# Fills ahead of the loads, 80-row loads, and batch 1's P v as 128-column matmuls, in a sparse attention with an ELU network behind it

## The chip, the cores and the metric

The kernel runs on one core of a Trainium2 chip. The metric is the time of one execution in microseconds (us) on the device, the median of the runs shown; less is better. The engines of the core are called PE (matmul; PEld is its weight load), DVE (elementwise), ACT (activation functions), POOL and SP; the last two issue most DMAs here.

## What is computed

Inputs are q, k and v, each (8, 8, 576, 64) in float32 (batch, head, position, channel), and two weight matrices of 512 x 2048 and 2048 x 512. The output is (4608, 512) in float32.

```python
stride = 32
scores = scale * np.matmul(q, k.transpose(0, 1, 3, 2))
mask_local   = (rel >= 0) & (rel < stride)                    # heads 0..3
mask_strided = (rel >= 0) & (pos[None] % stride == pos[:, None] % stride)   # heads 4..7
attn = softmax(np.where(masks, scores, -1e9))
x = np.matmul(attn, v).transpose(0, 2, 1, 3).reshape(4608, 512)
h = x @ w_in
g = np.where(h > 0, h, np.exp(np.minimum(h, 0)) - 1)          # ELU
out = g @ w_out
```

## The kernel before

Everything stays in SBUF as bf16. Attention is worked batch by batch (0 to 7). The four local heads are called `l`, the four strided ones `s`; a key such as `1s0` means batch 1, strided, pair 0, and each pair has two halves `u`. Positions are taken in eight residues s of 72 places p each (position 8p + s), so a load of one head brings 72 rows of 8 x 64 numbers. Strided scores are then 72 x 72 blocks, local ones 128 x 96 blocks (32 earlier keys and 96 own).

The network works on chunks of 512 tokens, of which there are nine. L1 gives for each of 16 blocks m four matmuls into one bank of PSUM (128 x 512), then ACT takes exp (`h`), DVE or ACT clamps it (`i`, `j`), and DVE takes the larger of that and h (`g`). L2 gives for each of four blocks of 128 tokens 16 matmuls in four parts (`Z`), then a copy out of PSUM (`o` on ACT, `q` on DVE) and the store (`t`).

The order of all work is a string of tokens, ORDER, written out by hand or by a planner; each token calls one function, and every engine takes its instructions in that order. Tokens that matter here:

- `F` fills (masks, zero pads, ones), `K` casts of the first two strided heads of batch 0 from a float32 stage, `T` transposes on PE for batches 0 to 2 (NPE = 3) with copies `c` (DVE) or `C` (ACT);
- `S` scores, `e` exp, `m` mask, `O` P v, `n` log of the row sums, `r` their reciprocal by exp, `x` the product into xT;
- `a`, `b` the two halves of an L1 block in chunk 0, `L` a whole one;
- `D` loads on POOL's queue, which also cast float32 to bf16; `V` copies the last 32 rows of each block of v for the local heads, `W` copies v for the strided heads into `vsp`;
- `X` DMA transposes and `P` pad copies into `kp` on SP's queue, from batch 3 on.

P v has two forms, chosen by OLDPV. The old one (batches 0 and 1) works with 64-column weights: for each half two matmuls with a block of ones for the row sums, and eight or six with v, the two heads of a pair in the two halves of the array; sums and products stand in two banks, 128 x 288 each. The new one (batches 2 to 7) works with 128-column weights in which 64 columns of v stand beside 64 columns of ones, so that one matmul gives products and sums together: 64 x 576 each. Its weights are `vsp` (strided) and `vl` (local, two buffers in turn); their ones are written once by the fills `F.vs`, `F.v0`, `F.v1`. They come as tokens at the head of ORDER, after the loads of batch 0 have been issued in the program's text; the fill of `vl0` therefore comes after the load into `vl0`.

Batch 1's raw rows are loaded into regions that are not in use yet, the tail of xT and part of g[1] (`raw1`). Batches from 3 on are transposed by DMA over 80 rows (RP), so rows 72 to 79 of the raw buffers must hold something finite; before, three small loads (`D.fqs`, `D.fks`, `D.fql`) put it there.

Of the kernel before, what the change touches and what calls it, by code (L numbers as in the profile page):

```python
# [8 lines left out]
F32 = mybir.dt.float32  # L9
BF16 = mybir.dt.bfloat16  # L10
# [5 lines left out]
S = 576  # L16
# [15 lines left out]
OLDPV = (0, 1)  # L32
# [3 lines left out]
w.7.42 F.ks0 F.ks1 F.kl0 F.v1 F.vs F.v0 F.kl1 F.ms K.q.1 F.ml D.wi0.0 K.q.0 K.k.0 D.wi1.0 T.0s0.q.0  # L36
K.k.1 c.0s0.q T.0s0.k.7 D.wi2.0 T.0s1.q.6 c.0s0.k c.0s1.q D.wi3.0 S.0s0.1.01 S.0s0.0.23 e.0s0.1
T.0s1.k.7 e.0s0.0 m.0s0.1 c.0s1.k m.0s0.0 S.0s1.1.67 S.0s1.0.01 D.qs.1 e.0s1.1 O.0s0.1.23 e.0s1.0
D.ks.1 m.0s1.1 O.0s0.0.67 n.0s0.1 m.0s1.0 T.0l0.q.0 r.0s0.1 n.0s0.0 x.0s0.1 O.0s1.1.45 r.0s0.0
c.0l0.q D.vs.1 T.0l0.k.3 x.0s0.0 n.0s1.1 r.0s1.1 T.0l1.q.6 c.0l0.k T.0l1.k.7 x.0s1.1 C.0l1.q D.ql.1  # L40
V.0 S.0l0.1.01 S.0l0.0.56 c.0l1.k e.0l0.1 O.0s1.0.34 e.0l0.0 m.0l0.1 S.0l1.0.01 n.0s1.0 m.0l0.0
O.0l0.1.56 e.0l1.0 D.kl.1 r.0s1.0 m.0l1.0 S.0l1.1.01 n.0l0.1 x.0s1.0 e.0l1.1 O.0l0.0.34 r.0l0.1
m.0l1.1 O.0l1.0.01 x.0l0.1 n.0l0.0 O.0l1.1.56 r.0l0.0 D.vl.1 n.0l1.0 x.0l0.0 a.0.1.7 r.0l1.0 n.0l1.1
x.0l1.0 a.0.0.4 r.0l1.1 a.0.3.0 x.0l1.1 b.0.1 D.wo0.0 b.0.0 h.0.1 b.0.3 h.0.0 i.0.1 a.0.7.5 h.0.3
g.0.1 a.0.4.6 j.0.0 b.0.4 i.0.3 a.0.8.7 g.0.3 D.wo1.0 h.0.4 a.0.12.3 i.0.4 b.0.12 g.0.0 a.0.13.0
h.0.12 b.0.13 D.wo2.0 g.0.4 a.0.14.4 h.0.13 i.0.12 b.0.14 g.0.12 j.0.13 T.1s1.q.6 a.0.6.1 D.wo3.0
c.1s1.q h.0.14 b.0.8 g.0.13 a.0.9.6 h.0.8 i.0.14 b.0.7 D.fqs.0 g.0.14 j.0.8 a.0.2.0 b.0.9 h.0.7
g.0.8 a.0.5.4 h.0.9 i.0.7 a.0.10.3 D.fks.0 i.0.9 b.0.6 g.0.7 a.0.15.7 h.0.6 b.0.2 g.0.9 D.fql.0
b.0.15 h.0.2 i.0.6 b.0.10 g.0.6 h.0.15 b.0.5 h.0.10 i.0.2 T.1s0.k.6 T.1s0.q.5 i.0.15 D.qs.2 h.0.5
T.1l0.q.1 i.0.10 C.1s0.q a.0.11.2 g.0.15 b.0.11 C.1l0.q g.0.2 T.1s1.k.7 h.0.11 T.1l0.k.5 g.0.10  # L50
T.1l1.k.0 C.1s0.k i.0.5 T.1l1.q.1 D.ks.2 C.1l0.k i.0.11 Z.0.1.0.3 c.1l1.k C.1l1.q C.1s1.k g.0.11
S.1l1.1.56 S.1s0.0.01 e.1l1.1 g.0.5 Z.0.3.0.7 e.1s0.0 m.1l1.1 V.1 D.ql.2 S.1s1.0.45 S.1s1.1.01
e.1s1.0 Z.0.1.1.3 m.1s0.0 e.1s1.1 m.1s1.0 O.1l1.1.45 m.1s1.1 O.1s1.0.01 n.1l1.1 Z.0.3.1.7 r.1l1.1
n.1s1.0 D.kl.2 x.1l1.1 Z.0.1.2.3 r.1s1.0 x.1s1.0 O.1s1.1.45 Z.0.3.2.7 n.1s1.1 r.1s1.1 O.1s0.0.01
x.1s1.1 D.vs.2 Z.0.1.3.3 n.1s0.0 r.1s0.0 D.vl.2 S.1l0.1.45 o.0.1 x.1s0.0 Z.0.3.3.7 e.1l0.1 t.0.1
S.1l1.0.01 m.1l0.1 o.0.3 S.1s0.1.23 S.1l0.0.45 Z.0.0.0.6 e.1l1.0 t.0.3 e.1l0.0 m.1l1.0 O.1l0.1.01
Z.0.0.1.6 e.1s0.1 m.1l0.0 n.1l0.1 m.1s0.1 O.1l0.0.23 r.1l0.1 O.1s0.1.45 x.1l0.1 n.1l0.0 Z.0.0.2.6
n.1s0.1 r.1l0.0 r.1s0.1 Z.0.0.3.6 x.1l0.0 x.1s0.1 O.1l1.0.01 o.0.0 T.2s1.k.2 W.2 Z.0.2.0.3 n.1l1.0
t.0.0 r.1l1.0 c.2s1.k Z.0.2.1.3 x.1l1.0 V.2 L.1.2.0 L.1.1.1 h.1.2 i.1.2 L.1.0.2 h.1.1 g.1.2 L.1.8.4
i.1.1 h.1.0 g.1.1 j.1.0 L.1.5.0 h.1.8 g.1.0 L.1.4.1 h.1.5 i.1.8 i.1.5 L.1.6.2 h.1.4 g.1.8 Z.0.2.2.3  # L60
i.1.4 h.1.6 g.1.5 j.1.6 Z.0.2.3.3 g.1.4 g.1.6 T.2s1.q.0 o.0.2 L.1.7.1 c.2s1.q t.0.2 S.2s1.0.23 h.1.7
T.2s0.k.0 T.2s0.q.4 e.2s1.0 i.1.7 T.2l1.q.5 D.qs.3 c.2s0.q C.2s0.k L.1.3.6 g.1.7 C.2l1.q D.ks.3
m.2s1.0 S.2s0.0.34 h.1.3 T.2l1.k.5 D.vs.3 e.2s0.0 O.2s1.0.01 i.1.3 L.1.9.7 c.2l1.k n.2s1.0 m.2s0.0
L.1.11.2 r.2s1.0 g.1.3 h.1.9 O.2s0.0.34 x.2s1.0 h.1.11 T.2l0.q.6 T.2l0.k.5 n.2s0.0 i.1.9 D.ql.3
c.2l0.q L.1.15.0 r.2s0.0 g.1.9 L.1.10.1 i.1.11 h.1.15 x.2s0.0 C.2l0.k S.2s0.1.67 g.1.11 S.2s1.1.34
h.1.10 L.1.14.5 X.ks.3 i.1.15 e.2s0.1 i.1.10 D.kl.3 e.2s1.1 L.1.13.2 g.1.15 h.1.14 g.1.10 S.2l1.1.34
h.1.13 L.1.12.0 i.1.14 X.qs.3 m.2s0.1 j.1.13 g.1.14 O.2s0.1.67 e.2l1.1 Z.1.0.0.1 g.1.13 n.2s0.1
D.vl.3 m.2l1.1 P.s.3 h.1.12 S.2l0.0.23 S.2l1.0.45 m.2s1.1 Z.1.0.1.1 r.2s0.1 i.1.12 e.2l1.0 g.1.12
Z.1.0.2.1 e.2l0.0 x.2s0.1 O.2s1.1.45 m.2l0.0 O.2l1.1.23 n.2s1.1 S.2l0.1.67 W.3 Z.1.0.3.1 n.2l1.1
X.kl.3 m.2l1.0 r.2s1.1 Z.1.1.0.0 o.1.0 x.2s1.1 Z.1.1.1.0 r.2l1.1 D.qs.4 X.ql.3 e.2l0.1 x.2l1.1  # L70
O.2l0.0.45 D.ks.4 Z.1.1.2.0 n.2l0.0 m.2l0.1 D.vs.4 O.2l0.1.67 r.2l0.0 S.3s1.0.23 t.1.0 Z.1.2.0.1
n.2l0.1 x.2l0.0 e.3s1.0 Z.1.1.3.0 r.2l0.1 m.3s1.0 O.3s1.0.23 x.2l0.1 o.1.1 S.3s1.1.45 Z.1.2.1.1
n.3s1.0 t.1.1 e.3s1.1 O.2l1.0.67 Z.1.3.0.0 r.3s1.0 m.3s1.1 P.l.3 n.2l1.0 x.3s1.0 O.3s1.1.45
Z.1.3.1.0 X.ks.4 r.2l1.0 n.3s1.1 S.3s0.0.23 x.2l1.0 Z.1.3.2.0 e.3s0.0 r.3s1.1 L.2.8.6 m.3s0.0
x.3s1.1 L.2.4.7 h.2.8 D.ql.4 i.2.8 O.3s0.0.45 h.2.4 L.2.10.2 g.2.8 n.3s0.0 i.2.4 L.2.2.3 h.2.10
g.2.4 r.3s0.0 L.2.9.6 i.2.10 h.2.2 g.2.10 L.2.5.7 D.kl.4 h.2.9 i.2.2 x.3s0.0 j.2.9 L.2.1.2 g.2.2
h.2.5 S.3l1.0.45 g.2.9 h.2.1 L.2.11.3 e.3l1.0 i.2.5 i.2.1 L.2.6.6 h.2.11 D.vl.4 g.2.5 X.kl.4
S.3l0.1.45 g.2.1 h.2.6 L.2.7.7 i.2.11 e.3l0.1 i.2.6 L.2.14.2 m.3l1.0 h.2.7 m.3l0.1 O.3l1.0.45 g.2.6
h.2.14 Z.1.3.3.0 g.2.11 n.3l1.0 L.2.15.6 i.2.7 r.3l1.0 i.2.14 g.2.7 o.1.3 L.2.0.3 h.2.15 x.3l1.0
t.1.3 L.2.3.7 h.2.0 i.2.15 g.2.14 O.3l0.1.45 h.2.3 L.2.13.0 g.2.15 n.3l0.1 i.2.3 L.2.12.2 i.2.0  # L80
r.3l0.1 g.2.3 h.2.13 Z.1.2.2.1 x.3l0.1 h.2.12 S.3l1.1.67 i.2.13 S.3l0.0.45 e.3l1.1 g.2.0 Z.1.2.3.1
X.ql.4 e.3l0.0 g.2.13 S.3s0.1.67 o.1.2 Z.2.1.0.3 m.3l1.1 m.3l0.0 e.3s0.1 i.2.12 O.3l1.1.01 Z.2.2.0.4
X.qs.4 m.3s0.1 n.3l1.1 g.2.12 O.3s0.1.67 r.3l1.1 Z.2.2.1.4 W.4 n.3s0.1 x.3l1.1 P.l.4 Z.2.2.2.4
r.3s0.1 x.3s0.1 Z.2.2.3.4 P.s.4 O.3l0.0.67 o.2.2 Z.2.1.1.3 t.1.2 n.3l0.0 Z.2.1.2.3 r.3l0.0 t.2.2
Z.2.0.0.4 x.3l0.0 L.3.4.7 D.qs.5 L.3.5.6 D.ks.5 h.3.4 i.3.4 L.3.3.5 D.vs.5 h.3.5 g.3.4 D.ql.5
L.3.9.0 i.3.5 h.3.3 g.3.5 j.3.3 S.4s1.0.12 L.3.11.7 h.3.9 g.3.3 e.4s1.0 L.3.0.6 i.3.9 h.3.11 m.4s1.0
S.4s0.0.12 g.3.9 h.3.0 X.ks.5 L.3.10.5 i.3.11 e.4s0.0 i.3.0 L.3.8.0 h.3.10 m.4s0.0 g.3.0 j.3.10
D.kl.5 O.4s1.0.12 Z.2.0.1.4 g.3.11 n.4s1.0 g.3.10 h.3.8 O.4s0.0.67 Z.2.0.2.4 r.4s1.0 i.3.8 n.4s0.0
g.3.8 L.3.6.5 x.4s1.0 r.4s0.0 D.vl.5 Z.2.0.3.4 h.3.6 x.4s0.0 L.3.2.2 i.3.6 o.2.0 g.3.6 S.4s1.1.01
t.2.0 h.3.2 L.3.13.4 e.4s1.1 i.3.2 X.kl.5 L.3.12.5 g.3.2 h.3.13 m.4s1.1 j.3.13 L.3.1.0 h.3.12 g.3.13  # L90
O.4s1.1.12 h.3.1 S.4l0.1.67 i.3.12 Z.2.3.0.4 n.4s1.1 g.3.12 e.4l0.1 Z.2.1.3.3 i.3.1 r.4s1.1 m.4l0.1
S.4l0.0.67 g.3.1 o.2.1 L.3.7.5 x.4s1.1 e.4l0.0 t.2.1 L.3.14.3 h.3.7 m.4l0.0 i.3.7 O.4l0.1.67 h.3.14
O.4l0.0.12 g.3.7 L.3.15.0 n.4l0.0 i.3.14 n.4l0.1 Z.2.3.1.4 g.3.14 r.4l0.0 Z.2.3.2.4 r.4l0.1 x.4l0.0
h.3.15 Z.2.3.3.4 x.4l0.1 i.3.15 S.4l1.0.12 o.2.3 Z.3.1.0.7 g.3.15 e.4l1.0 t.2.3 Z.3.1.1.7 m.4l1.0
O.4l1.0.01 S.4s0.1.23 n.4l1.0 S.4l1.1.45 Z.3.1.2.7 X.qs.5 e.4s0.1 r.4l1.0 Z.3.1.3.7 m.4s0.1 e.4l1.1
x.4l1.0 O.4s0.1.23 o.3.1 Z.3.0.0.6 P.s.5 m.4l1.1 n.4s0.1 W.5 O.4l1.1.01 X.ql.5 r.4s0.1 Z.3.0.1.6
n.4l1.1 D.qs.6 x.4s0.1 Z.3.0.2.6 r.4l1.1 D.ks.6 Z.3.3.0.7 P.l.5 x.4l1.1 D.vs.6 Z.3.0.3.6 t.3.1
S.5s1.1.01 o.3.0 S.5s1.0.23 S.5s0.0.45 e.5s1.0 L.4.3.6 t.3.0 e.5s1.1 m.5s1.0 L.4.2.3 e.5s0.0 m.5s1.1
D.ql.6 h.4.3 X.ks.6 O.5s1.1.01 m.5s0.0 O.5s1.0.45 h.4.2 i.4.3 L.4.7.2 n.5s1.0 g.4.3 Z.3.3.1.7
n.5s1.1 i.4.2 r.5s1.0 g.4.2 L.4.0.6 r.5s1.1 x.5s1.0 D.kl.6 h.4.7 L.4.9.3 x.5s1.1 h.4.0 O.5s0.0.45  # L100
i.4.7 h.4.9 S.5l1.0.01 i.4.0 Z.3.3.2.7 n.5s0.0 g.4.7 e.5l1.0 g.4.0 L.4.1.2 r.5s0.0 i.4.9 D.vl.6
m.5l1.0 S.5s0.1.01 h.4.1 L.4.13.6 x.5s0.0 P.s.6 e.5s0.1 i.4.1 O.5l1.0.45 g.4.9 h.4.13 S.5l0.1.01
X.qs.6 Z.3.3.3.7 n.5l1.0 m.5s0.1 i.4.13 e.5l0.1 L.4.8.3 g.4.1 r.5l1.0 g.4.13 O.5s0.1.12 o.3.3 X.kl.6
L.4.15.0 x.5l1.0 h.4.8 n.5s0.1 L.4.11.7 W.6 h.4.15 i.4.8 D.qs.7 S.5l0.0.45 m.5l0.1 r.5s0.1 t.3.3
Z.4.0.0.6 g.4.8 D.ks.7 h.4.11 x.5s0.1 L.4.4.3 e.5l0.0 D.vs.7 i.4.15 j.4.11 O.5l0.1.45 m.5l0.0 h.4.4
L.4.10.1 g.4.15 n.5l0.1 i.4.4 L.4.6.0 g.4.11 h.4.10 r.5l0.1 i.4.10 L.4.12.2 g.4.4 h.4.6 L.4.14.7
# [606 lines left out]
```

## Time and profile before

| | |
|---|---|
| time, median of 3 runs | 334.99 us (334.53 to 335.02) |
| the profiled execution | 334.41 us |
| its span in the trace | 332.7 us |
| PE, DVE, ACT, POOL busy | 307.3, 228.0, 234.4, 75.6 us |
| packets of the DMA queues | 99319, 38.61 MB |

The page of the profile gives, for one execution, the busy time of each engine, the span in 40 slices of 8.3 us, the chain that ended last, and groups of instructions by line and operation with their count, busy time and mean. A line of the trace in order of time has the start in us, the duration in us, engine, line, operation, output <- inputs, shape and count; in square brackets how long the engine had been idle before it and what ended that. A line of the waits has the total in us, the number of times and the longest. PE's busy time is modelled, since matmuls overlap in the array; the distance from the start of one to the start of the next says more.

### The profile page before, as it was taken

To read this page: it belongs to the slowest core of one execution; us is meant where nothing else is said; L and a number is where in the kernel's file an instruction comes from. 1 tells how busy PE (TensorE), PEld (TensorE's weight loads), DVE (VectorE), ACT (ScalarE), POOL (GpSimd) and SP (SyncE) were. 2 spreads that over 40 slices of the span, in tenths; PEclk is the share of its full clock that TensorE was granted. 3 is DMA by queue.
4 is the path that set the end of the run, shared out by engine and by line. 5 is a ranking of instruction groups with operands and counts; after the bars stand their busy time and mean duration, and the time that the engine had idled before them with its cause. 6 is when DMAs were issued, how large, how long until landed. Compare 5 with 4: busy or idle time off the path is not lost.

```text
span 332.7 us, 6428 instructions
## 1 busy us (share of the span) xinstructions
PE 307.3 (92%) x2410; PEld 158.8 (48%) x2410; DVE 228.0 (69%) x452; ACT 234.4 (70%) x408; POOL 75.6 (23%) x102
## 2 busy tenths in 40 slices
PE   5069999999989999999999999999999999999993
PEld 5056454446445445455554454455544444444441
DVE  5168796578966996788579979874589386447500
ACT  2038687868988897799799889689798675336320
POOL 8634230003920722630263205400000000000000
PEclk9999999999999999999999999999999999999998
DMA  7999997215999999999799989962400121111032
GB/s 148 187 206 188 206 196 69 65 32 92 155 183 140 184 134 180 169 94 141 155 208 129 175 152 157 110 163 61 131 14 0 35 62 32 33 34 53 10 92 69
DMA packets 99319, 38.61 MB, mean 116 GB/s; under 512 B 80568, under 2 KB 93112, under 8 KB 99288
## 3 DMA queue, kind: packets, MB, share of 16 engines
q0 software_dynamic: 65920, 18.66, 56.7%
q1 hardware_dynamic: 33128, 19.10, 27.1%
q10 hardware_dynamic: 240, 0.44, 0.4%
q8 instruction: 19, 0.31, 0.4%
q14 instruction: 12, 0.10, 0.1%
HBM read 37.84 MB, written 9.44 MB: 142 GB/s over the span
## 4 chain that ended last, share of the span: by engine, by line
PE 63%; DVE 12%; DMA 9%; ACT 8%; issue 4%; POOL 1%; SPq 0%; ACTq 0%; POOLq 0%; DVEq 0%
PE ps L636 30%; PE ps L602 25%; DVE g L630 4%; PE ps L440 3%; DVE he L619 3%; DMA kpl<-kTl 3%; DMA vl<-in_v_dram 3%; ACT e L447 3%; DVE xT L569 2%; DMA kTs<-ks 2%; ACT ln L538 2%; ACT he L610 2%; DMA kps<-kTs 2%; PE ps L510 1%; ACT rc L544 1%
## 5 line engine op out<-in xcount | busy, mean ns | idle before, releaser
L636 PE MATMUL ps<-w_out_sb,g 128*128 128x512 bf16 x576 | 136.6, 379 | 0.0
L602 PE MATMUL ps<-xT,w_in_sb 128*128 128x512 bf16 x576 | 135.1, 381 | 1.0 <-DVE g L630 0.8
L610 ACT ACTIVATE he<-ps 128x512 f32<-128x512 f32 x144 | 83.5, 595 | 31.8 <-PE ps L602 30.7
L602 PEld LDWEIGHTS <-w_in_sb 128*128 128x128 bf16 x576 | 54.5, 98 | 63.8 <-issue 4.7
L630 DVE TENSOR_TENSOR g<-he,ps 128x512 bf16<-128x512 bf16 x118 | 78.4, 681 | 6.4 <-PE ps L636 4.1
L636 PEld LDWEIGHTS <-g 128*128 128x128 bf16 x576 | 52.7, 98 | 56.3 <-DVE g L630 0.6
L619 DVE TENSOR_SCALAR he<-he 128x512 bf16<-128x512 f32 x118 | 50.9, 442 | 23.1 <-ACT he L610 22.4
L569 DVE TENSOR_TENSOR xT<-ps,rc 64x576 bf16<-64x576 f32 (+1 forms) x64 | 43.2, 679 | 23.2 <-ACT rc L544 22.3
L447 ACT ACTIVATE e<-ps 72x576 bf16<-72x576 f32 (+1 forms) x64 | 40.3, 647 | 18.0 <-PE ps L440 17.0
L538 ACT ACTIVATE ln<-ps 64x576 f32<-64x576 f32 (+1 forms) x64 | 36.9, 583 | 8.7 <-PE ps L510 6.2
L544 ACT ACTIVATE rc<-ln 64x576 f32<-64x576 f32 (+1 forms) x64 | 39.4, 620 | 1.5
L650 ACT COPY osb<-ps 128x512 f32<-128x512 f32 x32 | 18.7, 585 | 24.4 <-PE ps L636 24.3
L236 POOL DMA_DIRECT2D ql<-in_q_dram x20 | 16.5, 832 | 30.7 <-DMA qTl<-ql 27.9
L454 DVE TENSOR_TENSOR pm<-e,mask_s 72x576 bf16<-72x576 bf16 x32 | 14.4, 452 | 13.2 <-ACT e L447 12.8
L229 POOL DMA_DIRECT2D qs<-in_q_dram x7 | 5.5, 787 | 77.7 <-DMA qTs<-qs 45.3
L628 DVE SCALAR_TENSOR_TENSOR g<-he,ps 128x512 bf16<-128x512 bf16 x26 | 17.7, 680 | 1.1 <-ACT he L617 0.8
L460 DVE TENSOR_TENSOR pm<-e,mask_l 128x576 bf16<-128x576 bf16 x32 | 14.3, 453 | 4.5 <-ACT e L447 3.9
L617 ACT ACTIVATE he<-he 128x512 bf16<-128x512 f32 x26 | 16.4, 629 | 0.7
L243 POOL DMA_DIRECT2D kl<-in_k_dram x20 | 15.2, 776 | 5.8 <-DMA vs<-in_v_dram 2.8
L400 PE MATMUL ps<-identity,qs 72*128 72x72 bf16 x32 | 2.2, 226 | 12.8 <-DVE qs L387 12.8
L510 PEld LDWEIGHTS <-vl 128*128 128x128 bf16 x144 | 8.7, 96 | 6.4 <-issue 1.9
L503 PEld LDWEIGHTS <-vsp 72*128 72x128 bf16 x192 | 9.1, 98 | 5.4 <-issue 0.7
(91 smaller groups left out, 185.9 us busy)
## 6 DMA issues: line engine op xcount, KB each, us to landing
out_dram<-osb SPq DMA_DIRECT2D x31, 144.0 KB
vl<-in_v_dram POOLq DMA_DIRECT2D x8, 288.0 KB, 8.0
w_in_sb<-in_moe_w_in_dram POOLq DMA_DIRECT2D x4, 512.0 KB, 12.4
w_out_sb<-in_moe_w_out_dram POOLq DMA_DIRECT2D x4, 512.0 KB, 14.9
vs<-in_v_dram POOLq DMA_DIRECT2D x7, 288.0 KB, 7.5
qs<-in_q_dram POOLq DMA_DIRECT2D x6, 288.0 KB, 6.5
ks<-in_k_dram POOLq DMA_DIRECT2D x6, 288.0 KB, 8.6
kps<-kTs SPq DMA_DIRECT2D x10, 160.0 KB
```

Of the source, the lines that this page charges most:

```text
L236: nc.gpsimd.dma_start(out=t[0:RS, h % 2, :, h // 2, :], in_=q[b, h].rearrange("(p s) d -> p s d", s=NS))
L447: nc.scalar.activation(e[0:R], tiles.pop(("S", key, u))[0:R], ACT.Exp, scale=scale)
L538: nc.scalar.activation(t, s_ps, ACT.Ln)
L544: nc.scalar.activation(t, tiles.pop(("ln", key, u)), ACT.Exp, scale=-1.0)
L569: nc.vector.tensor_mul(dst, o_ps, rc)
L602: nc.tensor.matmul(tiles["h", ch, m], lhsT=w_in_sb[:, c, m * 128:(m + 1) * 128], rhs=xT[:, c, ch * CHUNK:(ch + 1) * CHUNK], start=(c == 2) ...
L610: nc.scalar.activation(e, tiles["h", i[0], i[1]], ACT.Exp)
L619: eng.tensor_scalar(e1, e, scalar1=1.0, scalar2=1.0, op0=ALU.min, op1=ALU.subtract)
L628: nc.vector.scalar_tensor_tensor(dst, e1, -1.0, h, op0=ALU.mult, op1=ALU.max)
L630: nc.vector.tensor_tensor(dst, e1, h, op=ALU.max)
L636: nc.tensor.matmul(ops, lhsT=g[ch % 2][:, m, kk * 128:(kk + 1) * 128], rhs=w_out_sb[:, m, :], start=(m == 0), stop=(m == MC - 1), skip_gro ...
L650: eng(o_sb, o_ps)
```

## The change

1. The fills of ones beside v in `vl0` and `vl1` stand in the program's text ahead of batch 0's loads of vs, ql, kl and vl, those of `vsp` and the zeros of `kp` right behind them; all are no tokens of ORDER any more. The large zero fills of `kp` go from DVE to ACT (a copy of a broadcast zero). POOL's iota goes ahead of its loads. `F.ml` makes two broadcast copies instead of six.
2. Loads of 72 rows take 80 rows, running eight rows into the next head (except at the very end of the tensor); the three small loads of rows 72 to 79 go. Both stage loads go to SP's queue.
3. Batch 1 takes the new form of P v: OLDPV is (0,), with one more copy `W.1`.
4. ORDER is written anew throughout. The number of tokens of each kind stays the same but for these: clamps on DVE 118 to 111 and on ACT 26 to 33, output copies on ACT 33 to 28 and on DVE 3 to 8, transposed copies on DVE 14 to 19 and on ACT 10 to 5.

```diff
-OLDPV = (0, 1)
+OLDPV = (0,)
 ORDER = """
-w.7.42 F.ks0 F.ks1 F.kl0 F.v1 F.vs F.v0 F.kl1 F.ms K.q.1 F.ml D.wi0.0 K.q.0 K.k.0 D.wi1.0 T.0s0.q.0
-K.k.1 c.0s0.q T.0s0.k.7 D.wi2.0 T.0s1.q.6 c.0s0.k c.0s1.q D.wi3.0 S.0s0.1.01 S.0s0.0.23 e.0s0.1
...
+w.7.42 F.ml K.q.0 D.wi0.0 K.q.1 F.ms T.0s0.q.0 D.wi1.0 K.k.0 c.0s0.q K.k.1 D.wi2.0 T.0s1.q.0
+T.0s0.k.1 c.0s1.q D.wi3.0 T.0s1.k.2 c.0s0.k c.0s1.k S.0s0.1.01 S.0s0.0.67 e.0s0.1 S.0s1.0.45
...
+    def runs(x, b, h, n):
+        rows = RP if (b * H + h + n - 1) * S + RP * NS <= B * H * S else RS
+        return rows, bass.AP(x.tensor, x.offset + (b * H + h) * S * D,
+                             [[NS * D, rows], [S * D, n], [1, NS * D]])
...
     def load_runs(nm, b, h0=0, n=HG):
         x = {"q": q, "k": k, "v": v}[nm[0]]
-        t = rawof(nm, b)
-        hb = (HG if nm[1] == "s" else 0) + h0
+        rows, in_ = runs(x, b, (HG if nm[1] == "s" else 0) + h0, n)
         nc.gpsimd.dma_start(
-            out=t[0:RS].rearrange("p (h f) -> p h f", h=HG)[:, h0:h0 + n],
-            in_=x[b, hb:hb + n].rearrange("h (p s) d -> p h (s d)", s=NS))
+            out=rawof(nm, b)[0:rows].rearrange("p (h f) -> p h f", h=HG)[:, h0:h0 + n], in_=in_)
...
-    load_stage(nc.sync, 0, q)
-    load_stage(nc.scalar, 1, k)
+    load_stage(0, q)
+    load_stage(1, k)
...
+    nc.gpsimd.iota(dist, pattern=[[1, RS]], base=RS, channel_multiplier=-1)
+    def fill_ones(t, n):
+        w = t.bitcast(F32)
+        nc.vector.memset(
+            w[:, 0:n * D].rearrange("p (n w d) -> p n w d", w=2, d=D // 2)[:, :, 0, :], two)
+        nc.vector.memset(w[:, n * D:], two)
+    for t in vl_t:
+        fill_ones(t, HG * LB)
+        nc.vector.memset(blocks(t, HG * LB)[0:PRE, 0, :], 0.0)
     for nm in ("vs", "ql", "kl", "vl"):
         load(nm, 0)
-    nc.gpsimd.iota(dist, pattern=[[1, RS]], base=RS, channel_multiplier=-1)
+    fill_ones(vs_p, HG * NS)
...
+    for (c, z), t in kp.items():
+        s_ = slice(2 * NS * RP, None) if c == "s" else slice(0, PRE)
+        nc.vector.memset(t[z * D:(z + 1) * D, s_], 0.0)
+        r = slice((1 - z) * D, (2 - z) * D)
+        w = t[r].bitcast(F32)
+        nc.scalar.copy(w, zero[r, 0:2].bitcast(F32).to_broadcast([D, w.shape[1]]))
...
-                for i in range(3):
-                    nc.vector.tensor_copy(mask_l[:, u, :, i, :], mask_1)
+                nc.vector.tensor_copy(mask_l[:, u],
+                                      mask_1.unsqueeze(2).to_broadcast([128, NS, 3, LN]))
```

## The prediction

> **What bounds the kernel now.** I read the page first (busy time, the 40 slices), then who waited for whom, then the instructions in order of time for the first 35 us, then the busy time by stretch.
>
> ```profile
> PE 307.3 (92%) x2410; PEld 158.8 (48%) x2410; DVE 228.0 (69%) x452; ACT 234.4 (70%) x408; POOL 75.6 (23%) x102
> ...
> PE   5069999999989999999999999999999999999993
> ...
> DMA  7999997215999999999799989962400121111032
> ```
>
> PE is the engine that works nearly throughout, but of its slices of 8.3 us the second is empty and the third at six tenths; the 5 of the first is warm-up on zeros (L381). Real work starts late. DMA is at 9 in the same slices. The waits say who is late:
>
> ```profile
> PE ps L400 <- DVE qs L387: 12.8, 1, 12.8
> ...
> DVE vl L347 <- DMA vl<-in_v_dram: 9.0, 1, 9.0
> ```
>
> PE's longest single wait is for a cast on DVE, and DVE's own longest is for the load of `vl`. In order of time:
>
> ```profile
> 5.45 1.20 POOL L253 DMA_DIRECT2D vl<-in_v_dram  x1
> 6.36 1.14 ACT L387 CAST ks<-g 72x512 bf16<-72x512 f32 x2 [3.61 <-DMA g<-in_k_dram]
> ...
> 7.20 0.31 POOL L312 TENSOR_SCALAR_AFFINE_SELECT mask<-mask 128x96 bf16<-128x96 bf16 x1
> ...
> 14.89 0.70 DVE L347 MEMSET vl<- 128x768 f32 x1 [8.95 <-DMA vl<-in_v_dram]
> ...
> 17.00 0.42 DVE L387 CAST qs<-g 72x512 bf16<-72x512 f32 x1
> ...
> 18.56 0.66 PE L400 MATMUL ps<-identity,qs 72*128 72x72 bf16 x8 [12.84 <-DVE qs L387]
> ```
>
> The load of `vl` is issued at 5.45; the fill F.v0, which writes ones beside v in the same buffer, stands behind it and waits until 14.89. The casts K.q, which need only the staged q, stand behind that fill on DVE. Staged k was there at 6.36 (ACT cast it then), and the mask at 7.51. So 18.56 is an accident of the order, not of the data.
>
> From the first L1 matmul (32.13) to the start of the last matmul (327.3) are 295.2 us. Priced by start-to-start distances in the rows (0.216 us for a 512-column matmul, 17.28 us for 80 on the chain; 0.24 to 0.26 for eight or six score, transpose or new P v matmuls; 0.38 for an old P v), the order after that point holds 281.8 us of PE slots. That leaves 13.4 us in which PE is not fed: 2.5 between 32.13 and the first L1 of chunk 1 at 67.74, 3.9 up to chunk 2 at 105.37, 7 in all the rest. PE is the bound there; what starts earlier ends earlier.
>
> **The change, part by part.**
>
> *Fills ahead of the loads.* New DVE order before the first cast: three memsets (0.4), two `vl` fills with their pads (2 x 0.92), `vsp` (1.00), the small memsets and pad strips (0.7), from 0.89 to about 5; then F.ml, which needs POOL's last mask select, 7.51 plus 0.21 for the iota now ahead of the loads: 7.7. Two copies of 288 columns instead of six of 96 (210 ns each): I take 0.5, giving 8.2; K.q.0 0.42; first transpose at 8.7 instead of 18.56. The large pad memsets (612 and 552 ns, two each) become ACT copies; the nearest ACT row with 576 f32 columns takes 0.64, so four end near 2.75 + 2.7 = 5.5, before staged k lands at 6.36: hidden; uncovered they would cost 2.7. Staged k now follows q on SP's queue (its issue takes 0.42), landing perhaps 0.5 later; K.k.0 comes after K.q.0 anyhow. The `vl` load now waits for its fill, done by 2.2, before POOL reaches it at 5.7; nothing behind it on POOL is held.
>
> *Is the data there?* POOL issues a load when the load eight before it has landed, so its starts give landings: kl at 13.0, vl 14.9, w_in parts 17.5 to 25.1, batch 1's five later loads 27.1 to 35.3, and w_out's parts 14.5 to 16.5 after their issues, 37.7 to 45.5. Batch 0's attention took 13.57 us (18.56 to 32.13), ACT-heavy; the same instruction counts (ACT 11.7 us instead of 11.3, at the same ratio) take 13.9, so L1 starts at 22.6. kl is wanted about 5.5 after the start (14.2), V.0's vl after 8.5 (17.2), the third w_in part at 24 (landed 22.5), the fourth at 27.5 (25.1). All fit, by 1 us at the least. First term: 32.13 to 22.6, **-9.5**.
>
> *80-row loads.* Each 288 KB load becomes 320 runs instead of 288. Five 72-row loads landed in 7.7 us (25.1 to 32.8), 1.54 each, while 512 equal runs of a w_in part took 2.6. Cost between nothing (80 rows spread over the 16 engines evenly) and 1.54 x 8/72 = 0.17 each; I take the upper end, as the queues are full then. Eight or nine loads up to batch 1's last, 1.4 us; batch 2's five more, 0.9; the three 32 KB row fills go (about 96 runs, -0.5). DMA ends its first run at about 57 instead of 55.4.
>
> [...]
>
> *Who needs these later landings.* By the busiest engine's work up to each token, at 93% (stage below), the new order asks for w_out's first part at 40.3 (39.1 with the 1.4 added), second 43.7 (41.5), third 47.0 (44.0), fourth 48.5 (46.9), batch 2's vs at 56 and vl at 58 (57). Margins of 1 to 3 us where before had 4 to 12. I charge **+1.0** for one that slips.
>
> *Batch 1's P v.* The old form to the next line, and the new (batch 2):
>
> ```profile
> 57.56 0.31 PE L467 MATMUL ps<-pm,ones 72*64 72x288 bf16 x2
> 57.70 0.30 PE L476 MATMUL ps<-pm,g 72*64 72x72 bf16 x8
> 57.93 1.04 PE L636 MATMUL ps<-w_out_sb,g 128*128 128x512 bf16 x4
> ```
> ```profile
> 95.61 0.42 PE L510 MATMUL ps<-pm,vl 128*128 128x96 bf16 x6
> 95.87 1.02 PE L636 MATMUL ps<-w_out_sb,g 128*128 128x512 bf16 x4
> ```
>
> 0.37 against 0.26 from start to start; about 0.12 less in each of eight: **-1.0** of PE slots, at the most (nothing where old ones stand side by side). The tail is paid elsewhere: 64x576 instead of 128x288 makes log 643 instead of 405 ns, reciprocal 679 instead of 443, write 753 instead of 456, eight each: ACT +3.8, DVE +2.4, and W.1 +0.68 on DVE (it waits for batch 1's vs, landed about 32, asked for at 33.4; behind it the elu of chunk 0).
>
> [...]
>
> *The rewritten order.* Counting tokens by mean durations, first L1 of chunk 0 to first of chunk 1: PE 33.1 to 34.0, DVE 28.3 to 33.7, ACT 30.2 to 33.1 us. Before, PE's 33.1 took 35.6 (93%). Three engines alike at 34 leave less room, but 93% of 34.0 is still 36.6: slack 2.6 for 2.5. Next stage: before ACT 35.5 in 37.6 (94%); now ACT 36.2, so 38.4 against 33.5 of PE: slack 4.9 for 3.9, **+1.0**. Later, PE remains the largest in nearly every stage (seven more clamps go to ACT, five output copies to DVE, both with room); I keep the 7 us, between 4 and 10.
>
> **Sum.** 8.7 + 13.9 + (281.8 - 1.0) + 13.4 + 1.0 + 1.0 = 318.8 to the last matmul, + 5.4 as before to the end: span 324.2 instead of 332.7. The profiled execution took 334.41, 1.7 outside its span: 325.9. The median of the runs is 0.6 above that execution: **326.5**, against 334.99.
>
> **Rivals.**
> *DMA is the bound of the first 60 us.* For: nine tenths busy through six slices, deadlines now 9 us earlier, bytes added. Against: L1 of chunk 0 needs only w_in, which lands before it. If the loads up to w_out's last part and vl of batch 2 come 4 to 7 us later than asked, the gain shrinks to 1.5 to 4.5: 329 to 333.5. Chance 0.13.
> *Slower: the pad copies.* From batch 3 on, scores wait for transposed k copied into `kp`; before, three waits of PE for these cost 1.6 in all. The chain shows 5.9 us for a `kps` copy and 9.5 for a `kpl`; the new order leaves 4 to 7 us of work between issue and first score in nearly all ten (before 3.5 to 20). At the mean landing each could stall PE for 1 to 2 us: +10 to 15, 336 to 341. It decides from 0.85 us a copy (8.5/10). Against: two of before's had under 4 us and no wait over 0.7. Chance 0.08.
> *The start isn't earlier.* If F.ml or a cast still meets a load (stage on one queue, or vl behind a late fill), the start stays above 16 and only the P v trade is left, -1 to +2: 334 to 337. Against: nothing ahead of K.q.0 now writes a loaded buffer. Chance 0.05.
>
> **Numbers.** 0.74 for the forecast, its own range 321.5 (slack 3 less, no charge for DMA or stage two) to 329 (slack 3 more). To hold eight in ten the range goes up into the first rival: 321.5 to 332. Faster by over 0.2% (0.7 us, what measurement can tell): 0.74 + 0.13 + 0.01 = 0.88; within: 0.03; slower: 0.09.
>
> **What would show it.** Right: DVE's fills end by 6 with no wait for `vl`; first L400 near 8.7; first L602 near 22.6; DVE, log and reciprocal rows of batch 1 as 64x576; L1 of chunk 1 near 59, of chunk 2 near 98. Wrong: PE waiting for `w_out_sb` or `xT` loads between 30 and 60 (first rival), L440 waiting for `kps` or `kpl` by more than 5 us in all (second), a first transpose after 12 (third); or PE gaps from 105 on that add up to over 10 us.

## The result, and the profile after

| | before | after |
|---|---|---|
| median of 20 runs each | 334.35 us | 333.49 us |
| lowest to highest | 333.48 to 338.29 | 329.94 to 337.72 |
| ratio, 95% interval | | 0.9943 (0.9917 to 0.997) |
| the profiled execution, its span | 334.41, 332.7 | 335.32, 333.6 |

The change makes the kernel about half a percent faster by the ratio, 2 us or so, and 0.9 us by the medians; 8.5 us had been forecast. Here and below the ratios leave out runs over 1.5% above the fastest of their kernel (six of after's 20) and the medians do not, so a ratio need not be the quotient of two medians. A profile shows one execution only: those of the changed kernel and of the experiments e3 and e4 lie 1.8, 3.2 and 0.4 us above their medians, those of e2, e6 and e7 lie 2.0, 1.7 and 1.9 us below.

In what follows "after" is the changed kernel; its scores are L438 (L440 before), L1 is L600 (L602), L2 is L634 (L636), pad copies L593 (L595). The page of after, the rows of PE and DMA and the granted clock:

```profile
PE 310.9 (93%) x2394; PEld 160.3 (48%) x2394; DVE 230.9 (69%) x448; ACT 239.3 (72%) x409; POOL 73.5 (22%) x99
...
PE   5889999999699959999989999999999999999993
...
PEclk9559999999799978999999999999999999999999
DMA  8999999639969992993999799525101220002122
```

The hole in slices two and three is gone: they went from 0 and 6 to 8 and 8. Two new holes have come, a 6 in the eleventh slice (83 to 92 us) and a 5 in the fifteenth (117 to 125). The clock of PE falls to 7 tenths in the first of them, and to 7 and 8 in the second and the slice behind it. It also stands at 5 in slices two and three, from 7.73 to 24.80 us. PE has 16 matmuls fewer and is busy 3.6 us longer.

The start, in order of time:

```profile
1.36 0.70 DVE L307 MEMSET vl<- 128x768 f32 x1
...
5.14 1.18 POOL L256 DMA_DIRECT2D vl<-in_v_dram  x1
...
7.42 0.88 DVE L385 CAST qs<-g 72x512 bf16<-72x512 f32 x2
...
8.03 0.75 PE L398 MATMUL ps<-identity,qs 72*128 72x72 bf16 x8 [2.92 <-DVE qs L385]
...
22.32 11.73 PE L600 MATMUL ps<-xT,w_in_sb 128*128 128x512 bf16 x48 [0.24 <-DVE xT L567]
```

The fill of `vl` stands ahead of its load, the cast follows the mask, and the first transpose comes at 8.03 instead of 18.56. L1 begins at 22.32, 9.8 us earlier, and PE has nearly no gap up to chunk 1, whose L1 begins at 59.73 (67.74 before). So 8.0 us are in hand at 60 us. At chunk 2 it is 4.4 (101.00 against 105.37), and from the start of chunk 1's L1 to the start of the last matmul after takes 268.5 us where before took 259.6. The waits say why:

```profile
PE ps L438 <- DMA kps<-kTs: 6.9, 4, 3.4
PE ps L398 <- DVE qs L385: 2.9, 1, 2.9
```

PE's longest waits are no more for a cast but for the pad copies of transposed strided k, four times; before they came to 1.0 us. No line of PE's waits names `w_out_sb`. PE around the two holes, in order of time (in the first column the start, then the duration; for several matmuls both are of the group):

```profile
81.64 1.90 PE L634 MATMUL ps<-w_out_sb,g 128*128 128x512 bf16 x8
85.19 0.21 PE L438 MATMUL ps<-qTs,kps 128*128 128x72 bf16 x1 [1.66 <-DMA kps<-kTs]
86.92 1.08 PE L438 MATMUL ps<-qTs,kps 128*128 128x72 bf16 x15 [1.52 <-DMA kps<-kTs]
87.81 1.90 PE L634 MATMUL ps<-w_out_sb,g 128*128 128x512 bf16 x4
...
117.92 0.42 PE L508 MATMUL ps<-pm,vl 128*128 128x96 bf16 x6
121.76 0.24 PE L438 MATMUL ps<-qTs,kps 128*128 128x72 bf16 x1 [3.42 <-DMA kps<-kTs]
122.33 0.60 PE L438 MATMUL ps<-qTs,kps 128*128 128x72 bf16 x7 [0.32 <-DMA kps<-kTs]
```

The first pair is batch 3, the second batch 4. After the waits of batch 3 four L2 matmuls start 0.42 to 0.43 us apart, where the eight ahead of them took the usual 0.216: PE runs at half speed there. The chain that ended last goes through both places, and shows where the copies come from:

```profile
79.91 0.55 SPq L593
80.46 0.05 issue
80.51 6.37 DMA kps<-kTs
...
105.09 6.81 DMA kl<-in_k_dram
111.90 0.02 SPq L587
...
111.96 2.00 SPq L587
...
114.06 0.54 SPq L593
114.60 0.04 issue
114.64 7.64 DMA kps<-kTs
```

Batch 3's copies were issued at 79.91 and wanted some 3.5 us later (the last L2 matmul ahead of the scores starts at 83.16), and were still under way at 86.88. Batch 4's (token `P.s.4`) were issued only at 114.06, since ahead of them on SP's queue stands the transpose of local k (`X.kl.4`), which waited for the load of `kl` until 111.96. The rows of strided k that `P.s.4` copies had their own transpose issued at 100.10.

### The profile page after: what moved, and what is told of

Same layout as the page of the kernel before. It is cut to its first block, busy times and chain, and to the rows that moved or that the text cites. A ratio compares the mean times of both kernels' runs of the same rounds, so it can differ in the third digit from the quotient of the medians.

```text
span 333.6 us, 6399 instructions
## 1 busy us (share of the span) xinstructions
PE 310.9 (93%) x2394; PEld 160.3 (48%) x2394; DVE 230.9 (69%) x448; ACT 239.3 (72%) x409; POOL 73.5 (22%) x99
## 4 chain that ended last, share of the span: by engine, by line
PE 51%; ACT 14%; DVE 11%; DMA 11%; issue 5%; POOL 4%; SPq 1%; ACTq 0%; DVEq 0%; POOLq 0%
PE ps L634 23%; PE ps L600 21%; ACT ln L536 5%; DMA kps<-kTs 4%; ACT rc L542 4%; DMA kl<-in_k_dram 3%; PE ps L438 3%; DVE g L628 3%; DVE xT L567 3%; ACT e L445 2%; DMA qTl<-ql 2%; ACT he L608 2%; DMA kTs<-ks 2%; POOL ql L239 2%; DVE he L617 2%
## 5 line engine op out<-in xcount | busy, mean ns | idle before, releaser
L634 PE MATMUL ps<-w_out_sb,g 128*128 128x512 bf16 x576 | 138.5, 385 | 0.1
L600 PE MATMUL ps<-xT,w_in_sb 128*128 128x512 bf16 x576 | 133.7, 381 | 1.6 <-DVE xT L567 0.6
L600 PEld LDWEIGHTS <-w_in_sb 128*128 128x128 bf16 x576 | 54.7, 98 | 64.8 <-issue 5.6
L634 PEld LDWEIGHTS <-g 128*128 128x128 bf16 x576 | 53.8, 99 | 58.1 <-issue 3.8
L628 DVE TENSOR_TENSOR g<-he,ps 128x512 bf16<-128x512 bf16 x111 | 74.2, 682 | 2.0
L567 DVE TENSOR_TENSOR xT<-ps,rc 64x576 bf16<-64x576 f32 (+1 forms) x64 | 45.3, 716 | 30.5 <-ACT rc L542 28.7
L617 DVE TENSOR_SCALAR he<-he 128x512 bf16<-128x512 f32 x111 | 48.0, 442 | 19.7 <-ACT he L608 19.2
L536 ACT ACTIVATE ln<-ps 64x576 f32<-64x576 f32 (+1 forms) x64 | 38.6, 615 | 7.3 <-PE ps L501 4.2
L648 ACT COPY osb<-ps 128x512 f32<-128x512 f32 x27 | 15.7, 585 | 28.8 <-PE ps L634 28.5
L626 DVE SCALAR_TENSOR_TENSOR g<-he,ps 128x512 bf16<-128x512 bf16 x33 | 22.3, 681 | 0.8 <-ACT he L615 0.5
L615 ACT ACTIVATE he<-he 128x512 bf16<-128x512 f32 x33 | 20.6, 628 | 0.7
L438 PE MATMUL ps<-qTs,kps 128*128 128x72 bf16 x160 | 8.7, 205 | 7.2 <-DMA kps<-kTs 6.9
L438 PEld LDWEIGHTS <-kps 128*128 128x128 bf16 x160 | 7.6, 104 | 10.7 <-DMA kps<-kTs 7.8
```

The costliest lines, as they stand in the source:

```text
L438: nc.tensor.matmul(dst, lhsT=kt[pr, k0:k0 + 128], rhs=rhs, start=True, stop=True, skip_group_check=True)
L536: nc.scalar.activation(t, s_ps, ACT.Ln)
L567: nc.vector.tensor_mul(dst, o_ps, rc)
L600: nc.tensor.matmul(tiles["h", ch, m], lhsT=w_in_sb[:, c, m * 128:(m + 1) * 128], rhs=xT[:, c, ch * CHUNK:(ch + 1) * CHUNK], start=(c == 2) ...
L617: eng.tensor_scalar(e1, e, scalar1=1.0, scalar2=1.0, op0=ALU.min, op1=ALU.subtract)
L626: nc.vector.scalar_tensor_tensor(dst, e1, -1.0, h, op0=ALU.mult, op1=ALU.max)
```

## The experiments

Theory A: the early start keeps its full worth, and what ate it are the waits for the pad copies of batches 3 and 4, with the half clock behind each. Rivals: B, the 80-row loads crowd the DMA engines; C, the new P v of batch 1 costs more than it saves; D, the rewritten order is worse as a whole, and the waits are only where this shows. Each run's time stands beside runs of the kernel before on the same chip; those had medians of 334.43 (e1 to e4), 334.55 (e5 to e8) and 335.47 (e9 to e11). Line numbers of e1, e5, e6 and e11 are 8 higher than those of after. The recorded expectations use letters of their own: their theory G is A here.

### The early start alone (e1), with 80 rows (e5), with the new P v (e6)

```diff
 e1: the kernel after, but with before's order and P v and 72-row loads
-OLDPV = (0,)
+OLDPV = (0, 1)
-        rows = RP if ... else RS
+        rows = RS
+    def fill_rows(nm): ...                 # the three small loads of rows 72 to 79
 ORDER of before without its fills at the head:
-w.7.42 F.ks0 F.ks1 F.kl0 F.v1 F.vs F.v0 F.kl1 F.ms K.q.1 F.ml D.wi0.0 K.q.0 ...
+w.7.42 F.ml F.ms K.q.1 D.wi0.0 K.q.0 ...
 e5: e1 with the 80-row loads, and without the three small ones
 e6: e1 with OLDPV = (0,) and W.1 ahead of V.1
```

> The old order of work with the early start alone: fills ahead of the loads, both stage loads on SP, the masks and casts first; 72-row loads with their row fills and the old P v for batch 1 stay. Theory G (the start's 10 us are real, and the new order gives them back later, at PE's waits for the pad copies of batches 3 and 4 and in the half clock after them): first transpose near 8, first L1 near 22.5, time 325 to 328, since the old distances between transposes, pads and scores are kept. Rival D (loads bound the stretch after 60 us, so that any earlier start waits there): 332 to 335, with PE waiting for loads or transposes between 40 and 120.

> The early start in the old order (e1, 324.9 us) with 80-row loads instead of 72-row loads and their three row fills. My term (up to 0.17 us more DMA for each load, none of it on the path while loads have 4 us or more of margin): 324 to 326. [...] Rival S (overlapping longer loads slow the transposes and pads): 326 to 329.

> The early start in the old order (e1, 324.9 us) with batch 1's P v in the new form and W.1 ahead of V.1. By the rows: PE 1.0 us less, ACT 3.8 and DVE 3.1 more in a stretch where PE is the fullest: 323.5 to 326. Rival P (ACT's log and reciprocal become the end of the chain there): 326 to 329, chunk 1's first L1 more than 1.5 us later than in e1. If the changed kernel with the old form (337.9 against 333.5) shows the form's own worth, 321 to 323.

Measured: e1 324.89 (ratio 0.9696, 0.9671 to 0.9722); e5 324.7 (0.9719, 0.9676 to 0.9761); e6 327.47 (0.9775, 0.9737 to 0.9813).

e1 takes the early start and nothing else, and gains 9.5 us; its first transpose comes at 9.62, not near 8 as expected, since the strided mask still stands ahead of the casts. In its trace every stage lies 8.1 to 9.0 us ahead of before's, to the last matmul (318.3 against 327.3): PE is the bound all the way, and nothing behind the start gives the gain back. e5 is e1 within the intervals: 80-row loads cost nothing that can be measured, and B falls. e6 is 2.6 us slower than e1 (the ratios differ by 0.0079), and 2.8 slower than e5. Its waits of PE hold two that e1 has not:

```profile
PE ps L509 <- ACT e L453: 0.8, 1, 0.8
PE ps L406 <- DVE xT L575: 0.9, 1, 0.9
```

A P v matmul waits for its exp, and transposes wait for DVE's product, 1.7 us together. That ACT and DVE are late because of the tails with 64 partitions (in before a log over 64x576 took 643 ns and one over 128x288 405, a write 753 and 456) fits this, but is not shown to be the 2.6: the profile of e6 is of its fastest run and that of e1 of its slowest, and in these two traces the last matmul starts at 318.45 and 318.34. So by the times C holds in before's order, and where the loss lies is open; whether C holds in the new order as well, e4 and e10 ask.

### The pads ahead of their scores (e2, e7, e8, e9)

```diff
 e7: P.s.4 ahead of X.kl.4
-... O.3l0.0.67 X.kl.4 L.2.7.5 ... D.ks.5 P.s.4 L.2.8.3 ...
+... O.3l0.0.67 P.s.4 X.kl.4 L.2.7.5 ... D.ks.5 L.2.8.3 ...
 e2: e7, and batch 3's first scores behind three parts of L2
-... g.1.13 S.3s0.1.45 m.2l1.0 D.qs.4 S.3s0.0.12 g.1.15 ... Z.1.1.2.7 ... Z.1.1.3.7 ... Z.1.0.2.3 ...
+... g.1.13 m.2l1.0 g.1.15 Z.1.1.2.7 Z.1.1.3.7 Z.1.0.2.3 S.3s0.1.45 D.qs.4 S.3s0.0.12 ...
 e8: the load of vl for batch 3 behind that of vs for batch 4, not ahead of it
-... P.s.3 D.vl.3 i.1.12 ... D.vs.4 m.3s0.0 ...
+... P.s.3 i.1.12 ... D.vs.4 D.vl.3 m.3s0.0 ...
 e9: e7 and e8 together
```

> The changed kernel with two moves in its order: P.s.4 ahead of X.kl.4 on SP's queue, and batch 3's first two score tokens behind Z.1.1.2, Z.1.1.3 and Z.1.0.2 (2.6 us of PE work). Theory G: PE's waits for kps shrink from 6.9 us to under 2, the clock stays full between 60 and 130, time 324 to 327. Rival D: the waits turn up at other loads or transposes, time 331 to 334. A rival between: only batch 4's wait goes (it is a queue's order), batch 3's stays (it is the transposes' own time): 328 to 330.

> The changed kernel with P.s.4 ahead of X.kl.4 and nothing else. Theory G: batch 4's wait (3.4 us of PE and the half clock behind it) is SP's order and goes; batch 3's (3.3 us and one window of half clock) stays; time 329 to 331, about half way from 333.5 to 328.9. If batch 4's pads are late for another reason: 332 to 335 with the wait for kps near 120 still there.

> The changed kernel with the two loads of batch 3's vl moved on POOL's queue behind batch 4's qs, ks and vs, so that they no longer run while batch 3's pad copies do. Theory C (the pad copies take 5 to 8.5 us because those loads' small runs stand in the same DMA engines): batch 3's first scores start near 85 instead of 86.9, wait for kps 2 us less, clock full there, 329 to 332. If the pads' own time is the bound: first scores near 87 as before, 332 to 335.

> The changed kernel with both moves: batch 3's vl loads behind batch 4's first loads (e8 took away batch 3's wait, and batch 4's grew by as much) and P.s.4 ahead of X.kl.4 (e7 took away batch 4's). Theory G with C: no wait for kps over 1 us, full clock from 24 us on, the stage from chunk 1 to chunk 2 about 37 us as in e8 and from chunk 2 to chunk 3 about 32 as in e7: 324 to 326.5, that is the forecast's own sum. If something else takes the gain: 328 to 331.

Measured: e2 328.91 (0.9816, 0.9785 to 0.9847); e7 329.33 (0.985, 0.981 to 0.9889); e8 334.18 (0.9973, 0.9944 to 1.0002); e9 325.16 (0.9702, 0.967 to 0.9733).

e7 moves one token and gains some 3 us on after: `P.s.4` is issued at 104.70, the score of batch 4 comes at 116.77 with no wait, and only batch 3's waits are left. e8 alone gains nothing that can be told from after. Its time missed (329 to 332 was expected), but what was expected at batch 3 came. Batch 3's pads, with no `vl` load beside them, come in time, and batch 4's are waited for as much longer, since they still stand behind `X.kl.4` and the load of `kl`:

```profile
82.97 0.21 PE L438 MATMUL ps<-qTs,kps 128*128 128x72 bf16 x1
83.55 0.66 PE L438 MATMUL ps<-qTs,kps 128*128 128x72 bf16 x15 [0.37 <-DMA kps<-kTs]
...
120.15 0.24 PE L438 MATMUL ps<-qTs,kps 128*128 128x72 bf16 x1 [6.19 <-DMA kps<-kTs]
```

Chunk 2 begins at 96.33 instead of 101.00, and the wait of batch 4 has grown from 3.42 to 6.19. The first hole had in part covered the second. In e2, whose batch 3 asks for its pads later, both waits are gone as well (no line of PE's waits names `kps`), and the clock is full from 23.4 us on. Its median of 328.91 still lies above the 324 to 327 expected; the profile is of its fastest run (326.94), so what the slower ones met is not shown.

With both mended and the scores left in their place (e9) the waits for these copies are 0.3 us in all, the clock is full from 23 us on, and the order as changed gives what it had in it:

```profile
PE   5789999999899999899899999999999999999993
PEclk9559999999999999999999999999999999999999
```

D falls as the cause of the loss: moving two tokens of ORDER makes the new order as fast as e1. e9's 325.16 is 1.3 us from the forecast's 326.5, in part by luck: neither of the forecast's two charges of 1.0 shows in it, as is said below.

These traces also price the half clock, for the same order runs with and without it. From the second score of batch 3 to chunk 2's L1 is 12.78 us in e7 (86.78 to 99.56), in e8 (83.55 to 96.33) and in e9 (83.67 to 96.45), all at full clock there, although e7 had waited 1.77 and 1.07 us just before; in after it is 14.08 (86.92 to 101.00). That is 1.30 us for one stretch of half clock. From batch 4's first score to chunk 3's L1 it is 15.02 in e7 and e9 and 17.84 in after, where a second pad copy takes 0.32 of the difference: 2.5 us for the stretch there (e8, which has a stretch of the same length at its own wait, takes 17.97). The stretches in after, by windows (width, busy time and count of PE, PEld, DVE, ACT, POOL, then the granted clock, DMA share and GB/s):

```profile
86.20:89.65 3.45, 2.73 (x21) 1.63 (x22) 0.91 (x2) 1.18 (x2) 0.00 (x0) 0.51 1.23 202
120.37:127.19 6.82, 5.10 (x19) 2.17 (x20) 1.22 (x2) 1.33 (x2) 0.00 (x0) 0.50 0.73 82
```

Now the loss can be added up. At chunk 3's L1 after (139.60) is 10.75 us behind e9 (128.85): 3.25 up to batch 3's second score, of which 0.8 are there at chunk 1 already (the half clock of the start lasts to 24.80 in after and to 23.11 in e9, and the first 48 matmuls of L1 take 11.73 and 10.92) and some 2.4 are the waits; 1.30 of half clock; 3.38 up to batch 4's first score, the wait; 2.82 behind it, half clock and a pad. In all about 6 us of waits and 4.6 of clock. Some of it comes back later: at the last matmul 9.3 are left (328.2 against 318.9), between the medians 8.3.

### PE kept busy in the waits (e3)

```diff
+... w.4.45 S.3s0.1.45 ...      # 45 matmuls on zeros ahead of batch 3's first scores
+... w.6.45 S.4s0.0.67 ...      # and of batch 4's
```

> The changed kernel with 45 matmuls on zeros (about 2.5 us) ahead of the first scores of batch 3 and of batch 4, into the bank that those write next; nothing else moves. They fill idle time. Theory G, with the half clock as the larger half of the loss: waits for kps as long as before in sum with the zeros, but the clock stays full, time 328 to 331. If the waits alone are the loss and the clock is only a sign of them: 333 as the changed kernel. If the zeros don't count as work: the clock falls as before, 333 to 336.

Measured: 333.1 (0.9919, 0.9885 to 0.9953), no better than after. It missed, since the scores waited behind the zeros as well:

```profile
84.06 2.68 PE L379 MATMUL ps<-zero 128*128 128x128 bf16 x45
86.57 0.20 PE L438 MATMUL ps<-qTs,kps 128*128 128x72 bf16 x1
88.97 0.66 PE L438 MATMUL ps<-qTs,kps 128*128 128x72 bf16 x15 [2.21 <-DMA kps<-kTs]
```

The second copy, issued 0.5 us later than in after, came 2 us later (8.6 us from the issue, not 7.0), so work on PE did not shorten it. The clock stayed full at batch 3: from the second score to chunk 2's L1 it is 12.78 again (88.97 to 101.75). At batch 4 waits of 1.75 and 0.35 us and one stretch of half clock (124.86 to 128.27) were left. So with the zeros the clock stayed full at one place of two, and the scores came no sooner.

### The old P v in the new order (e4, e10)

```diff
 e4: after with the old P v for batch 1; e10: e9 with the same edit
-OLDPV = (0,)
+OLDPV = (0, 1)
-... h.0.7 W.1 b.0.12 ...
+... h.0.7 b.0.12 ...
```

> The changed kernel with batch 1's P v in the old form again (ones and v apart, W.1 gone), in the same order otherwise. Theory G: L1 of chunk 1 within 1.5 us of 59.7 (PE 1 us more, ACT 3.8 and DVE 3.1 less), time 332 to 335, the pad waits unchanged. Rival P (the new form's dearer log, reciprocal and write are what ate the gain): 325 to 329, with chunk 1 starting at 56 or sooner.

> As e9, with batch 1's P v in the old form (no W.1). In the old order the new form cost 2.6 us (e6 against e1). If that is the form's own price: 322 to 324.5, 2 to 3 below e9. By the rows for PE alone: 1 us above e9. If e6's loss is the order not made for it: within 1 us of e9.

Measured: e4 337.93 (1.0022, 0.998 to 1.0064, against after's 0.9943); e10 327.05 (0.9758, 0.9724 to 0.9792).

Beside e9 on the same chip e10 is 1.9 us slower (327.05 against 325.16; the runs do not overlap): in this order the new form gains 1.9. The same form cost 2.6 in before's order (e6). So its worth depends on the order; that the new order puts the tails of batch 1 where ACT and DVE have room is a likely reason, but only argued. The traces do not give the 1.9 to the form alone: e10 is 1.5 behind e9 at chunk 1, of which 1.0 is half clock at the start (it lasts to 25.17, and the first 48 matmuls of L1 take 11.91 against 10.92), it then waits 1.1 us more for batch 3's pads, and it is 0.8 behind at the last matmul. e4 missed (332 to 335 was expected): its chunk 1 begins at 59.8 as in after, but its waits for pads are 8.6 instead of 6.9. Why they are longer there was not followed up.

### A version that beats both (e11)

```diff
 e11: e5 with the casts ahead of the strided mask, and the vl load of batch 3 behind vs of batch 4
-w.7.42 F.ml F.ms K.q.1 D.wi0.0 K.q.0 K.k.0 ...
+w.7.42 F.ml K.q.0 K.q.1 F.ms D.wi0.0 K.k.0 ...
-... n.2s0.1 D.vl.3 m.2l1.1 P.s.3 ... D.vs.4 O.2l0.1.67 ...
+... n.2s0.1 m.2l1.1 P.s.3 ... D.vs.4 D.vl.3 O.2l0.1.67 ...
```

> The early start in the old order with 80-row loads (e5, 324.7 us), the casts ahead of F.ms, and batch 3's vl loads behind batch 4's first loads. First transpose at 8 instead of 9.2, batch 3's wait for kps (1.7 us in e5) gone: 321.5 to 324. If the vl loads now slow the kpl copies that follow instead: 324 to 326, with PE waiting for kpl near 103.

Measured: 322.89 (0.9626, 0.9592 to 0.966), 12.6 us less than before beside it and 2.3 less than e9. It has the early start, 80-row loads, the old P v in batch 1 and the old order with one load moved. So the rewriting of ORDER was not needed for the gain. No wait for `kps` is left among its scores of batch 3. What is next late there:

```profile
PE ps L446 <- DMA kpl<-kTl: 2.4, 2, 1.4
```

## Why the prediction was wrong

**The start: right.** The first transpose came at 8.03 (8.7 forecast), the first L1 at 22.32 (22.6), chunk 1's at 59.73 (59). The term was -9.5; at the first L1 it is -9.8, and e1, which has this term and no other, is 9.5 faster by the medians and 8.9 ahead at the last matmul. The third rival falls, and so does the first: w_out and batch 2's loads were there when asked for.

**80-row loads, and the charge for a load that slips: too dear by 1.0.** e5 against e1 shows neither a cost nor a gain (324.7 against 324.89); PE is the bound there, so a load that lands a little sooner or later need not show in the time. The other +1.0, for ACT in the stage from chunk 1 to chunk 2, was not needed either: that stage was to take 38.4 us and takes 37.5 in e9 (58.94 to 96.45).

**Batch 1's P v: right in sign, the size open.** -1.0 was forecast as the most; e10 against e9 gives -1.9 by the medians, with half clock at the start and a wait for pads in it, and e6 against e1 gives +2.6 in the other order. That the tail is paid on ACT and DVE was said; that this makes the difference is not shown.

**The later order: the step that failed.** The prediction put it so: "Later, PE remains the largest in nearly every stage [...]; I keep the 7 us, between 4 and 10." It weighed busy times by stage, and by these it was right: the new order holds no more PE work and e9 runs it from chunk 1 to the last matmul in 260.0 us, before in 259.6. But busy times say nothing of when a copy is issued, and the step put nothing down for waits on the pad copies or for a lower clock. Two copies of ten were late: the scores waited 6.9 us for them, half clock behind the waits cost some 3.8 more, and from chunk 1 on after took 268.5 us.

**The second rival was the case, and it was sized wrongly.** It named the mechanism, the sign of it ("L440 waiting for `kps` or `kpl` by more than 5 us in all": 6.9 and 0.7) and got a chance of 0.08. Three things of it failed. It spread 1 to 2 us over all ten copies; eight cost next to nothing and two cost 3.2 and 3.7 us. It left out the half clock that came behind both waits in after: 1.30 and 2.5 us, not far from half of what the waits cost. And "4 to 7 us of work between issue and first score" was counted as if a copy were issued when its token's turn comes, and as if its length were given. For batch 4 the turn itself came late, behind a transpose that waits for a load 6.8 us long; e7, which only moves `P.s.4` past it, takes this wait away. For batch 3 there were some 3.5 us from issue to score, fewer than the 4 to 7, and the copies took 5.3 and 7.0; e8, in which the `vl` load is issued at 84.25 instead of beside them, has them in 4.1 and 4.7 at most.

**"Two of before's had under 4 us and no wait over 0.7"** was the argument against the rival. Before's batch 3 shows how thin that was: its copies were issued at 91.91, with the `vl` load just ahead of them as in after, and its scores waited until 97.97 and 98.49, 6.1 and 6.6 us after the issue. The trace of before thus had the length of such a copy, 6 us beside a load; set against 3.5 us in the new order it gives the first wait, about 3 us, before any run.

Half clock could have been weighed too, but the page of before hides it. Its row of the granted clock is full to the last slice because the records of the clock begin at 33.96 us there, and what lies ahead of them counts as full (1.00 from 0 to 33.96). The matmuls show half speed up to that point. The same 42 matmuls on zeros, before and after:

```profile
1.06 4.66 PE L381 MATMUL ps<-zero 128*128 128x128 bf16 x42 [1.06 <-DVE zero L299]
1.06 4.05 PE L379 MATMUL ps<-zero 128*128 128x128 bf16 x42 [1.06 <-DVE zero L295]
```

In before they start 0.107 us apart throughout; in after, whose records begin with full clock at 4.32, the last ones start 0.056 apart. The first five matmuls of before's L1 start 0.40, 0.43, 0.43, 0.43 and 0.29 apart, and from 34.1 us on 0.216. The prediction took these as part of the 2.5 us in which "PE is not fed" up to chunk 1. So before's trace had the price of a matmul at half clock; what a pause in the middle of the run does, none of its rows showed.

What decides whether half clock comes with a wait is not shown. In after it came for 3.41 us with waits of 1.66 and 1.52 us, one short matmul between them, and for 6.83 us with a wait of 3.42; in e3 for 3.41 us with waits of 1.75 and 0.35. e7's waits of 1.77 and 1.07 left the clock full, and so did e3's of 2.21. Neither the longest wait nor the sum parts these cases: e7's two are longer than e3's 1.75 and 0.35. In the 3.41 us ahead of after's three falls of the clock up to 130 us, at 7.73, 86.24 and 120.37, PE was busy, by the modelled ends of its matmuls, for 0.79, 0.92 and 1.38 us, so a stretch without any matmul was not needed. From 0.427 and 0.216 us from start to start at half and at full clock, 3.41 us of half clock would cost, as an estimate, up to 1.7 us; measured were 1.30, and 2.5 for 6.83.

**The spread.** After's 20 runs span 7.8 us, e9's six 1.2. Of after's, the sixteen with a mean granted clock of 0.955 to 0.972 get shorter as the clock gets higher, from 335.6 and 336.0 at 0.955 to 329.94 at 0.972; four with 0.977 to 0.987 (331.0 to 337.7) do not fit this. They may be runs whose records of the clock begin late, as in the traces of e4 to e7 (at 23.6 to 24.0 us): e4 has half clock at the same two places as after, for the same lengths, and a mean of 0.981 where after has 0.957. Why the clock differs from run to run was not shown.

## What to carry to other kernels

When a bound engine starts earlier, list each transfer that something on it waits for, and set the time between issue and use in the new order against the longest landing seen in the trace under the same traffic; take the issue from the queue, that is from what the instruction ahead of it waits for, and not from the token's place. A wait on TensorE can cost its clock besides, here 1.3 and 2.5 us: waits of 1.66 and 1.52 us together and of 3.42 (after) came with half clock, waits of 1.77 and 1.07 (e7) and of 2.21 (e3) did not. The profile's row of the granted clock does not show a stretch that lies ahead of the first record of the clock (33.96 us in before); the distances between matmuls do (0.107 us there between those on zeros, 0.056 at full clock in after). When mending one of two such places gains nothing, look whether the next wait has grown by as much, and mend both in one run.

## What was not expected of the hardware

- The same pad copy (two DMAs, issued together by SP) had both parts landed within 4.7 us of the issue in e8 and 5.0 in e10, where the `vl` load comes later, 7.0 in after beside the `vl` load, and 8.2 for batch 4 in after, issued at 114.06. What lengthened batch 4's copy was not tested.
- Half clock came in stretches of 3.41, 6.83, 13.65 (the start of e9) and 17.07 us (the start of after), one, two, four and five times the same length; that of batch 3 in after begins at 86.24, inside the second pause.
- Loads of 80 rows instead of 72 made no difference to the time: 324.7 us (e5) against 324.89 (e1).
